# Spectral mixing with three real products: a complex product rebuilt inside a pipelined kernel

## The chip, the core and the metric

The kernel runs on one core of a Trainium2 chip. The metric is the device time of one execution in microseconds (us). A core has a matrix engine (TensorE, in the profile PE for products and PEld for weight loads), a vector engine (VectorE, DVE), a scalar engine (ScalarE, ACT), a general engine (GpSimd, POOL) and SyncE (SP), which here only starts transfers. Each engine works through its own list of instructions in order. Products land in PSUM, which this kernel uses as banks of 512 fp32 columns; everything else lies in SBUF.

## The reference, cut to what matters

```python
def _attn_ref(x, w_r, w_i, b_r, b_i):            # x: 4 batches x 3008 x 256
    X = np.fft.rfft(x, axis=1)
    Xr, Xi = X.real, X.imag
    Yr = Xr @ w_r - Xi @ w_i + b_r               # the mixing: a complex product
    Yi = Xr @ w_i + Xi @ w_r + b_i
    lam = 0.01                                   # soft threshold on both parts
    Yr = np.sign(Yr) * np.maximum(np.abs(Yr) - lam, 0.0)
    Yi = np.sign(Yi) * np.maximum(np.abs(Yi) - lam, 0.0)
    return np.fft.irfft(Yr + 1j * Yi, n=x.shape[1], axis=1)

def _moe_ref(x, w_in, w_out, a, b):              # x: 12032 x 256, 2048 hidden
    h = x @ w_in
    P = a[0] + a[1] * h + a[2] * h**2 + a[3] * h**3
    Q = 1.0 + np.abs(b[0]) * np.abs(h) + np.abs(b[1]) * h**2
    return (P / (Q + 1e-06)) @ w_out
```

The output of the first function, flattened to 12032 rows, is the input of the second.

## The kernel before

The transform of length 3008 is split into 47 x 64. For one batch there are these tasks: eight `f1_task` (the first factor, then a trip through DRAM, `s1`), and then twelve times, for a pair p of frequencies, `f2_task` (the second factor), `m_task` (the mixing with the threshold) and `i1_task` (the first step back, written to DRAM, `s2`). The last step back, `i2_task`, belongs to the second half of the kernel: it makes one block of up to 470 columns of the expert layer's input.

Numbers are kept to nearly fp32 by splitting them into a high and a low fp32r part and multiplying high x high, high x low and low x high (three products); some products are made in plain fp32.

**The mixing.** `f2_task` leaves four pieces of 128 columns in one bank (two frequencies k, two halves dc of the 256 features; in each piece 64 real and 64 imaginary columns). ACT copies the bank to the high part of `x` (L252), DVE subtracts to get the low part (L255), and DVE writes the negated imaginary columns in front of the real ones (L259), so that `-Xi | Xr` can be read as one block of 128 columns. `m_task(b, p, k)` then makes, for one frequency k, twelve products of 256 columns (L283): with `w_r` against `Xr | Xi` and with `w_i` against `-Xi | Xr`, two halves each, three split products each. Its result has real and imaginary rows under each other (64 + 64) and k side by side in the bank. The bank was filled with the two biases beforehand, by a product in batch 0 (L276) and by an ACT copy of `offset` for batches 1 to 3 (L155). After k = 1, ACT (L289) and DVE (L292) apply the threshold and leave `yt`, which `i1_task` multiplies in fp32 by `g1`, two products of 256 columns (L301), whose 128 contracted rows are the real and imaginary rows of one frequency.

**The expert layer** runs over 208 units: 26 blocks of columns by 8 pairs of hidden slices. A unit has 12 products into `h` (`g1_mm`, L385), three passes of ACT over `h` (L417, L418, L421), one adding transfer started by POOL (L419), the polynomial and the quotient on DVE (L433, L434, L442, L444, L454), one subtraction on POOL (L448), and 12 products into `acc` (`g2_mm`, L475), three units later.

**The order.** Batch 0 goes through its tasks before the units start. Those of batches 1 to 3 are laid into the units by a small planner in the main loop. Each task carries `(cost, use, free, generator, part)`; the planner sums the costs that are left and the known cost of each unit up to the batch's deadline (the last unit before its first block), makes a level from them, and at step "F" of each unit starts tasks until the unit's budget is spent. A generator is driven on at later steps: step "e" for tasks of part 0, steps "h"/"m" and the end of the unit for tasks of part 1. What a task must hand to a transfer it appends to `late`, and `flush()` at the start of the next unit issues it on SP. The kernel's last 64 units hold no such tasks; there `alone` is set, and `i2_task` makes the low part with a product (L357) and an ACT copy (L359) instead of DVE's subtraction (L362).

```python
        while cur and spent + cur[0][0] / 2 < budget and held + cur[0][1] <= 2 and not (live and storing(i)):
            cost, use, free, g, part = cur.pop(0)
            next(g, None)
```

Two PSUM banks (tag `ft`) are shared by `f1`, `f2`, mixing, `i1` and `i2`. `h` has two pairs of banks, `acc` two banks.

Of the kernel before, what the change touches and what calls it, by code (L numbers as in the profile page):

```python
# [37 lines left out]
def dft_tables():  # L38
    n2 = np.arange(N2)
    k2 = np.arange(NK)  # L40
    n1 = np.arange(N1)
    k1 = np.arange(N1)
    w = 2.0 * np.pi / N2
    ang = w * ((n2[:, None] * k2[None, :]) % N2)
    f1 = np.zeros((ROWS, NK, 2))
    f1[:N2, :, 0] = np.cos(ang)
    f1[:N2, :, 1] = -np.sin(ang)
    i2b = np.zeros((NK, NG, 2, NG, N2))
    i2 = np.zeros((NK, 2, N2))
# [32 lines left out]
    sel = np.zeros((4, 130))  # L82
    sel[0:2, 0:64] = 1.0
    sel[2:4, 64:128] = 1.0
    sel[0::2, 128] = 1.0
    sel[1::2, 129] = 1.0
    f = np.float32
# [12 lines left out]
def spectral_moe(ctx, tc, t, out):  # L100
# [14 lines left out]
    offset = const.tile([128, 2, D], F32, name="offset")  # L115
    minus = const.tile([128, 128], F32R, name="minus")
    wmix = {n: const.tile([128, 2, D], F32R, name=n) for n in ("wrh", "wrl", "wih", "wil")}
# [20 lines left out]
    def load_x(b, c):  # L138
        if b == 1 and c in (2, 3):
            xt = pro3.tile([128, 4, D], F32, tag=f"x{c}", name="xin", bufs=1)  # L140
        elif b == 1 and c >= 6:
            xt = sm.tile([128, 6, D], F32, tag="x", name="xin", bufs=2)[:, :4]
# [42 lines left out]
    def f1_task(b, c, pos):  # L185
# [11 lines left out]
        elif b > 1:  # L197
            whole = sm.tile([128, 3, 2, D], F32, tag="x", name="a", bufs=2)[:, :NG]
# [41 lines left out]
    def f2_task(b, p):  # L240
# [10 lines left out]
        xs = (sm if b else pro3).tile([128, 2, 4, 192], F32R, tag="x", name="x", bufs=2 if b else 3)  # L251
# [6 lines left out]
        if b or p < 2:  # L258
# [8 lines left out]

    def m_task(b, p, k):
# [4 lines left out]
        if k == 0 and copied:  # L273
            copy(0, pt, offset)
        elif k == 0:
            nc.tensor.matmul(out=pt, lhsT=selr, rhs=bias, start=True, stop=False, skip_group_check=True)  # L276
# [61 lines left out]
    def i2_task(n, ec):  # L338
# [8 lines left out]
        for i in range(JB):  # L347
            z = slice(i * TJ, 512 if i == JB - 1 else (i + 1) * TJ)
# [141 lines left out]
    def fft_tasks(b):  # L490
# [4 lines left out]
        for p in range(np_ + 2):  # L495
# [4 lines left out]
            if 1 <= p <= np_:  # L500
                ts += [(1.43, 1 - k, k, m_task(b, p - 1, k), 0) for k in range(2)]
# [32 lines left out]
    with tc.manual_schedule():  # L534
# [5 lines left out]
        nc.vector.memset(offset[:, 0], 0.0)  # L540
        idle = offset[:, 0].bitcast(mybir.dt.bfloat16)
# [9 lines left out]
        sel = pro.tile([4, 130], F32, tag="sel", name="sel", bufs=1)  # L551
# [11 lines left out]
        def prepare_small():  # L563
            nc.vector.memset(v32(selr), 0.0)
            nc.vector.memset(v32(bias), 0.0)
            yield
            nc.vector.tensor_copy(selr[:4], sel[:, 0:128])
            nc.scalar.activation(out=minus, in_=eye, func=ACTF.Copy)
# [81 lines left out]
        for p in range(np_ + 3):  # L650
# [84 lines left out]
        for i in range(-1, nu + 4):  # L735
# [3 lines left out]
            freed = 0  # L739
            if i == 3:  # L740
# [6 lines left out]
            for step in order.replace("m", "").replace("2", "2m").replace("1A", "Ao1") if nextb == B and not cur else order:  # L747
                if step == "F":
# [14 lines left out]
                    if cur:  # L763
                        budget += plan.pop(0) if plan else level
                        while cur and spent + cur[0][0] / 2 < budget and held + cur[0][1] <= 2 and not (live and storing(i)):
                            cost, use, free, g, part = cur.pop(0)
                            next(g, None)
                            (parts if part else live).append(g)
# [3 lines left out]
                            if not cost:  # L772
# [16 lines left out]
                elif step == "e":  # L789
                    for g in live:  # L790
# [7 lines left out]
            if 0 <= i < nu:  # L798
                dve_a(i)
            next(prev, None)  # L800
# [51 lines left out]
```

## Time and profile before

| | |
|---|---|
| time, median of 3 runs | 1433.52 us (1431.99 to 1437.6) |
| the profiled execution, device time | 1429.0 us |
| its span in the profile | 1427.2 us |
| PE busy / weight loads | 1404.7 us (98%) / 1232.4 us (86%) |
| DVE busy | 1294.8 us (91%) |
| ACT busy | 1135.6 us (80%) |
| POOL busy | 668.9 us (47%) |

How to read it: the profile is of one execution. Busy time is the time in which at least one instruction of the engine is recorded as running. A matmul's record is longer than the distance to the next one's, since they are pipelined, so the chain of waits, which counts from start to start, is the better measure of what a matmul costs. Three stretches can be told apart: batch 0 and the constants (up to about 100 us), units with transform tasks laid in (to about 1060 us), and units without (to the end).

### The profile page before, as it was taken

What the parts mean: (1) busy time and instruction counts of PE and PEld (TensorE: products, weight loads), DVE (VectorE), ACT (ScalarE), POOL (GpSimd) and SP (SyncE); (2) the same over time, 40 slices, a digit from 0 to 9 for tenths busy, and PEclk for the clock granted to TensorE, in tenths of its full rate; (3) what the DMA queues carried; (4) which work ended last, traced back from release to release, by engine and by line L of the source; (5) the groups of instructions that cost most, each with busy time, mean ns of one, the idle gap of its engine ahead of it and who ended that gap; (6) DMA issues with size and microseconds to landing.
All of it is one profiled execution on the core that took longest, in us unless ns stands there. A gap on an engine that the chain in (4) does not pass through costs nothing.

```text
span 1427.2 us, 20352 instructions
## 1 busy us (share of the span) xinstructions
PE 1404.7 (98%) x7525; PEld 1232.4 (86%) x7525; DVE 1294.8 (91%) x1298; ACT 1135.6 (80%) x1439; POOL 668.9 (47%) x444
## 2 busy tenths in 40 slices
PE   9988999999999999999999999999999999999997
PEld 5966999999878999998888999999988888888887
DVE  3868889989899889999889999999999999999998
ACT  3768777788887787878888787888788998888985
POOL 0533444445454444454454444445455555555553
PEclk9999999999999999999999999999999999999999
DMA  9958445546686455546586455555455555555543
GB/s 333 383 189 170 103 104 129 114 89 148 141 205 160 108 108 117 110 102 142 134 213 153 96 122 108 115 116 108 92 124 112 106 115 103 110 113 105 113 80 79
DMA packets 84374, 191.58 MB, mean 134 GB/s; under 512 B 8556, under 2 KB 40468, under 8 KB 84276
## 3 DMA queue, kind: packets, MB, share of 16 engines
q0 software_dynamic: 29952, 98.58, 38.7%
q1 hardware_dynamic: 54212, 91.67, 19.3%
q8 instruction: 59, 0.97, 0.3%
q14 instruction: 39, 0.32, 0.1%
q10 hardware_dynamic: 112, 0.05, 0.0%
HBM read 54.21 MB, written 37.49 MB: 64 GB/s over the span
## 4 chain that ended last, share of the span: by engine, by line
PE 77%; DVE 11%; issue 8%; DMA 2%; ACT 2%; SPq 0%; DVEq 0%; ACTq 0%
PE h L385 29%; PE acc L475 29%; PE pft L283 7%; PE pi L351 4%; DVE t L433 3%; DVE v L444 3%; PE pft L247 2%; PE pft L301 2%; DVE g L442 1%; PE pft L191 1%; PE pft L174 1%; DVE t L434 1%; DVE g L454 1%; PE pm L283 1%; DVE e L525 1%
## 5 line engine op out<-in xcount | busy, mean ns | idle before, releaser
L475 PE MATMUL acc<-g,wsp 128*128 128x470 f32 (+1 forms) x2496 | 562.4, 374 | 3.4 <-DVE g L454 3.4
L448 POOL TENSOR_TENSOR t<-t,v 128x940 f32<-128x940 f32 (+1 forms) x206 | 478.5, 2323 | 137.8 <-DVE v L444 121.5
L475 PEld LDWEIGHTS acc<-g,wsp 128*128 128x128 f32 x2496 | 469.9, 190 | 62.5 <-DVE g L454 4.3
L385 PE MATMUL h<-xsh,win 128*128 128x470 f32 (+1 forms) x1664 | 433.3, 382 | 6.1 <-DVE t L434 5.6
L419 POOL DMA_DIRECT2D v<-s x208 | 183.6, 883 | 538.9 <-issue 501.3
L385 PEld LDWEIGHTS h<-xsh,win 128*128 128x128 f32 x1664 | 304.1, 190 | 61.6 <-PE acc L475 10.9
L417 ACT ACTIVATE v<-h 128x940 f32<-128x940 f32 (+1 forms) x208 | 196.1, 943 | 148.5 <-PE h L385 143.8
L442 DVE SCALAR_TENSOR_TENSOR g<-t,small,y 128x940 fp32r<-128x940 f32 (+1 forms) x208 | 255.2, 1227 | 51.1 <-ACT y L428 48.8
L433 DVE TENSOR_TENSOR t<-t,h 128x940 f32<-128x940 f32 (+1 forms) x208 | 231.4, 1112 | 24.7 <-ACT t L421 22.8
L434 DVE SCALAR_TENSOR_TENSOR t<-t,small,h 128x940 f32<-128x940 f32 (+1 forms) x208 | 245.2, 1179 | 7.4
L454 DVE SCALAR_TENSOR_TENSOR g<-t,small,y 128x940 fp32r<-128x940 f32 (+1 forms) x208 | 244.1, 1174 | 0.1
L385 PE MATMUL h<-xsl,win 128*128 128x470 f32 (+1 forms) x832 | 242.3, 373 | 0.0
L444 DVE SCALAR_TENSOR_TENSOR v<-v,g 128x940 f32<-128x940 f32 (+1 forms) x208 | 231.7, 1114 | 0.0
L421 ACT ACTIVATE t<-h,small 128x940 f32<-128x940 f32 (+1 forms) x208 | 215.6, 1036 | 0.0
L426 ACT ACTIVATE y<-v 128x940 f32<-128x940 f32 (+1 forms) x208 | 205.7, 989 | 8.1 <-DMA v<-s 8.0
L428 ACT ACTIVATE y<-y 128x940 f32<-128x940 f32 (+1 forms) x208 | 203.9, 980 | 2.4
L418 ACT ACTIVATE s<-h 128x940 f32<-128x940 f32 (+1 forms) x208 | 195.3, 939 | 0.0
L385 PEld LDWEIGHTS h<-xsl,win 128*128 128x128 f32 x832 | 156.1, 188 | 19.9
L283 PE MATMUL pft<-wrh,x 128*128 128x256 f32 x288 | 76.7, 288 | 0.2 <-ACT pft L155 0.2
L283 PE MATMUL pft<-wih,x 128*128 128x256 f32 x288 | 75.1, 283 | 0.0
L351 PEld LDWEIGHTS pi<-small,ct 96*128 96x128 f32 x516 | 65.7, 192 | 5.5 <-ACT a L155 3.0
L351 PE MATMUL pi<-small,ct 96*128 96x94 f32 (+1 forms) x516 | 66.9, 277 | 2.1 <-DMA ct<-s 2.1
(90 smaller groups left out, 1070.8 us busy)
## 6 DMA issues: line engine op xcount, KB each, us to landing
v<-s POOLq DMA_DIRECT2D x192, 470.0 KB, 4.5
xin<-in_x SPq DMA_DIRECT2D x30, 512.0 KB, 6.5
s<-zt SPq DMA_DIRECT2D x48, 256.0 KB, 3.5
out_t<-ob SPq DMA_DIRECT2D x48, 235.0 KB, 4.5
ct<-s SPq DMA_DIRECT2D x20, 480.0 KB, 5.5
bt<-s SPq DMA_DIRECT2D x36, 256.0 KB, 3.9
s<-a SPq DMA_DIRECT2D x42, 192.0 KB, 5.2
v<-s POOLq DMA_DIRECT2D x16, 376.0 KB, 4.0
```

Of the source, the lines that this page charges most:

```text
L283: nc.tensor.matmul(out=pt[:, k, :], lhsT=l, rhs=r, start=False, stop=n == len(ops) - 1, skip_group_check=True)
L385: nc.tensor.matmul(out=h[:, i, :w], lhsT=l, rhs=r, start=k == 0, stop=k == len(halves) // FU - 1)
L421: nc.scalar.activation(out=d["t"], in_=h, func=ACTF.Identity, scale=rate["a3"], bias=ca[:, 2:3])
L426: nc.scalar.activation(out=d["y"], in_=d["v"], func=ACTF.Square, bias=C0)
L428: nc.scalar.activation(out=d["y"], in_=d["y"], func=ACTF.Abs_reciprocal_sqrt)
L433: nc.vector.tensor_tensor(out=tt, in0=tt, in1=h, op=ALU.mult)
L434: nc.vector.scalar_tensor_tensor(out=tt, in0=tt, scalar=ca[:, 1:2], in1=h, op0=ALU.add, op1=ALU.mult)
L442: stt(out=hi, in0=tt, scalar=ca[:, 0:1], in1=y, op0=ALU.add, op1=ALU.mult)
L444: stt(out=v, in0=v, scalar=C0, in1=v32(hi), op0=ALU.add, op1=ALU.mult)
L448: nc.gpsimd.tensor_tensor(out=tt[:, :cut], in0=tt[:, :cut], in1=v[:, :cut], op=ALU.subtract)
L454: stt(out=lo, in0=tt, scalar=ca[:, 0:1], in1=y, op0=ALU.add, op1=ALU.mult)
L475: nc.tensor.matmul(out=acc[n][e][:, :w], lhsT=l, rhs=r, start=begun[n] == 1 and seen[e] == 1, stop=begun[n] == UB and seen[e] == 3 * FU)
```

## The change

For batches 1 to 3 the complex product is made from three real ones: with S = (Xr + Xi) w_r, the real part is S - Xi (w_r + w_i) and the imaginary part S + Xr (w_i - w_r). The first of them is made in plain fp32 by a task of its own, `m_sum`: ACT lays `offset` (now `b_r` on all 128 rows) into the first half of a bank, two fp32 products of 256 columns add S, and ACT copies that half to the other half. `m_rest` adds the difference of the biases to the second half by one product (`apart`, `bias`) and then the two other real products in split form, twelve products of 256 columns. Both frequencies k now lie on the rows and the real and imaginary parts side by side, the other way round than `i1_task` needs them, and four transfers of 64 x 256 per pair (`turn`, on SP) bring `yt` to `y`. `f2_task` writes its columns grouped by real and imaginary part; DVE makes the sum and the negated copy is gone. The two new weight matrices are made in unit 0 (`join_mix`) from `w_r` and `w_i`, which are loaded once more during batch 0. In `i2_task` the last product of a block in the stretch without tasks is 94 columns instead of 136. The planner's costs of the two new tasks are 0.86 and 1.56 where the two old ones had 1.43 each, and starting an `m_sum` ends a unit's list of new tasks. Batch 0 keeps `m_task`.

```diff
@@ f2_task
-        pt = bank(b, "f2" if p % 2 else "").rearrange("p (z f) -> p z f", z=4)
+        bank_ = bank(b, "f2" if p % 2 else "")
+        pt = bank_.rearrange("p (z f) -> p z f", z=4)
+        slots = bank_.rearrange("p (c d k j) -> p c d k j", c=2, d=2, k=2)
...
-                nc.tensor.matmul(out=pt[:, 2 * k + dc, :], lhsT=bt[:, k, dc * 128:(dc + 1) * 128],
+                nc.tensor.matmul(out=slots[:, :, dc, k, :] if b else pt[:, 2 * k + dc, :], lhsT=bt[:, k, dc * 128:(dc + 1) * 128],
...
+        if b:
+            total = sm.tile([128, 256], F32, tag="sum", name="total")
+            xs = sm.tile([128, 4, 256], F32R, tag="x", name="x")
+            flat = xs.rearrange("p z f -> p (z f)")
+            nc.scalar.activation(out=total, in_=bank_[:, :256], func=ACTF.Copy)
+            nc.scalar.activation(out=flat[:, :512], in_=bank_, func=ACTF.Copy)
+            yield
+            yield
+            nc.vector.tensor_tensor(out=total, in0=bank_[:, 256:], in1=total, op=ALU.add)
+            nc.vector.tensor_tensor(out=flat[:, 512:], in0=bank_, in1=v32(flat[:, :512]), op=ALU.subtract)
+            yield
+            x_t[b, p] = xs, total
+            return
...
+    def m_sum(b, p):
+        assert copied and not both
+        pt = m_t[b] = bank(b, "m").rearrange("p (c d) -> p c d", c=2)
+        total = x_t[b, p][1]
+        copy(0, pt[:, 0], offset)
+        for dc in range(2):
+            nc.tensor.matmul(out=pt[:, 0], lhsT=total[:, dc * 128:(dc + 1) * 128], rhs=wr[:, dc, :],
+                             start=False, stop=False, skip_group_check=True)
+        both.append(lambda: copy(0, pt[:, 1], pt[:, 0]))
+        yield
+        while both:
+            both.pop()()
+
+    def m_rest(b, p):
...
+        ops = [(1, apart, bias[:, 1])]
+        for c, wh, wl in ((1, "wnh", "wnl"), (0, "wdh", "wdl")):
+            for dc in range(2):
+                ah, al = (xs[:, 2 * z + c, dc * 128:(dc + 1) * 128] for z in range(2))
+                ops += [(1 - c, ah, wmix[wh][:, dc, :]), (1 - c, ah, wmix[wl][:, dc, :]), (1 - c, al, wmix[wh][:, dc, :])]
+        for n, (o, l, r) in enumerate(ops):
+            nc.tensor.matmul(out=pt[:, o], lhsT=l, rhs=r, start=False, stop=n == len(ops) - 1, skip_group_check=True)
+        yield
...
+        def turn():
+            y_t[b, p] = y = sm.tile([128, 2, D], F32, tag="yt", name="y")
+            for k in range(2):
+                for c in range(2):
+                    nc.sync.dma_start(out=y[64 * c:64 * c + 64, k], in_=yt[64 * k:64 * k + 64, c])
+
+        late.append(turn)
+
+    def join_mix(wi):
+        wd = sm.tile([128, 2, D], F32, tag="b", name="wd")
+        nc.vector.tensor_tensor(out=wd, in0=wi, in1=wr, op=ALU.subtract)
+        nc.vector.scalar_tensor_tensor(out=wi, in0=wr, scalar=-1.0, in1=wi, op0=ALU.mult, op1=ALU.subtract)
+        yield
...
+            nc.scalar.activation(out=wmix[h], in_=w, func=ACTF.Copy)
+        yield
+        for w, h, l in ((wi, "wnh", "wnl"), (wd, "wdh", "wdl")):
+            nc.vector.tensor_tensor(out=wmix[l], in0=w, in1=v32(wmix[h]), op=ALU.subtract)
@@ i2_task
-            z = slice(i * TJ, 512 if i == JB - 1 else (i + 1) * TJ)
+            z = slice(i * TJ, 512 if i == JB - 1 and not alone[n] else (i + 1) * TJ)
@@ fft_tasks
-                ts += [(1.43, 1 - k, k, m_task(b, p - 1, k), 0) for k in range(2)]
+                ts += [(0.86, 1, 0, m_sum(b, p - 1), 2), (1.56, 0, 1, m_rest(b, p - 1), 0)]
@@ batch 0, p == 8
-                for k, nm in enumerate(("b_r", "b_i")):
-                    for z in range(2):
-                        nc.sync.dma_start(out=offset[64 * k:64 * k + 64, z],
-                                          in_=t[nm].rearrange("(o d) -> o d", o=1).to_broadcast([64, D]))
+                nc.sync.dma_start(out=offset, in_=t["b_r"].rearrange("(o d) -> o d", o=1).to_broadcast([128, D]))
+                nc.sync.dma_start(out=wr, in_=t["w"][:, 0])
+                w_i = sm.tile([128, 2, D], F32, tag="b", name="w_i")
+                nc.sync.dma_start(out=w_i, in_=t["w"][:, 1])
@@ planner
-                            if not cost:
+                            if not cost or part == 2:
                                 break
```

On PE, in the first half of batch 1's pairs, the mixing of one pair stood as two tasks with a unit's products between them (`h` and `acc` are the units' own products):

```order
L283 MATMUL pft<-wrh,x 128x256
L283 MATMUL pft<-wrl,x 128x256
L283 MATMUL pft<-wrh,x 128x256
L283 MATMUL pft<-wih,x 128x256
L283 MATMUL pft<-wil,x 128x256
L283 MATMUL pft<-wih,x 128x256
L283 MATMUL pft<-wrh,x 128x256
L283 MATMUL pft<-wrl,x 128x256
L283 MATMUL pft<-wrh,x 128x256
L283 MATMUL pft<-wih,x 128x256
L283 MATMUL pft<-wil,x 128x256
L283 MATMUL pft<-wih,x 128x256
```

These are the twelve rows of one frequency; the twelve of the other follow a unit later, or directly. Now, on PE in the same part of the kernel, the start of a mixing reads as follows (L295 the two fp32 products, L457 and L547 the unit's `h` and `acc`, L313 the product for the biases and the first split ones):

```order
L253 MATMUL pft<-f_70,bt 128x2x64 x4
L295 MATMUL pft<-wr,total 128x256 x2
L457 MATMUL h<-xsh,win_489 128x470 x4
L457 MATMUL h<-xsl,win_489 128x470 x2
L457 MATMUL h<-xsh,win_489 128x470 x4
L457 MATMUL h<-xsl,win_489 128x470 x2
L547 MATMUL acc_2296<-g,wsp_1062 128x470 x4
L547 MATMUL acc_2297<-g,wsp_1062 128x470 x4
L547 MATMUL acc_2296<-g,wsp_1062 128x470 x2
L547 MATMUL acc_2297<-g,wsp_1062 128x470 x2
L313 MATMUL pft<-bias,apart 128x256
L313 MATMUL pft<-wnh,x 128x256
```

Eleven more split products follow in the same unit. Between `m_sum` and `m_rest` there is always at least one unit's worth of `h` and `acc`.

On SP, at batch 1's first pairs, this is what stood in its list before (bt: a load for `f2`; s: a store of `i1`; ct: a load for `i2`; out_t: the output):

```order
L227 DMA bt<-s_990 128x2x256 x5
L308 DMA s_1571<-zt 128x2x256
L329 DMA ct<-s_402 96x1280
L227 DMA bt<-s_990 128x2x256 x2
L308 DMA s_1571<-zt 128x2x256
L484 DMA out_t<-ob 128x470 x2
```

And this is what stands at the same place now (y: the turning transfers):

```order
L231 DMA bt<-s_994 128x2x256 x5
L325 DMA y<-yt 64x256 x4
L401 DMA ct<-s_406 96x1280
L325 DMA y<-yt 64x256 x4
L380 DMA s_1669<-zt 128x2x256
L556 DMA out_t<-ob 128x470 x2
L231 DMA bt<-s_994 128x2x256
L325 DMA y<-yt 64x256 x4
L380 DMA s_1669<-zt 128x2x256
```

Per pair, four more entries stand in SP's list, each group behind the DVE instruction that finishes `yt` and, from the second pair of a batch on, behind the previous pair's `i1` products, which read the buffer that `y` takes.

## Rows read from the trace of the kernel before

**Rows 1.** The page's busy times: engine, us, share of the span, instructions.

```profile
PE 1404.7 (98%) x7525; PEld 1232.4 (86%) x7525; DVE 1294.8 (91%) x1298; ACT 1135.6 (80%) x1439; POOL 668.9 (47%) x444
```

**Rows 2.** Busy time of each engine by stretch, and the clock.

```profile
core 0: us, PE busy (x) PEld busy (x) DVE busy (x) ACT busy (x) POOL busy (x), PEclk, DMA share, GB/s
150.00:1050.00 900.00, 900.00 (x4940) 802.78 (x4940) 823.13 (x808) 721.21 (x912) 418.95 (x270) 1.00 0.57 126
900.00:950.00 50.00, 50.00 (x290) 46.79 (x290) 47.86 (x50) 41.14 (x53) 24.04 (x18) 1.00 0.53 112
1150.00:1200.00 50.00, 49.68 (x241) 43.36 (x240) 49.35 (x46) 44.78 (x53) 27.57 (x18) 1.00 0.54 107
```

**Rows 3.** The chain of waits, 264 to 300 us: start, us, what.

```profile
267.39 1.43 PE pft L283 x12
268.82 2.59 PE h L385 x12
271.41 2.57 PE acc L475 x12
273.98 0.86 PE pft L301 x4
274.84 0.89 PE pft L247 x8
...
280.88 1.42 PE pft L283 x12
```

**Rows 4.** Who waited for whom, 150 to 1060 us: total us, times, longest.

```profile
DVE g L442 <- ACT y L428: 48.8, 61, 2.3
...
ACT pft L155 <- DVE xsl L362: 15.3, 8, 2.1
...
ACT pft L155 <- DVE x L255: 12.8, 5, 3.2
PEld h L385 <- DVE v L444: 7.3, 9, 0.8
```

**Rows 5.** Groups by line: shape, count | busy us, mean ns | idle before.

```profile
L255 DVE TENSOR_TENSOR x<-pft,x 128x512 fp32r<-128x512 f32 x48 | 32.7, 682 | 0.8 <-ACT x L252 0.8
...
L155 ACT ACTIVATE pft<-offset 128x512 f32<-128x512 f32 x36 | 21.8, 606 | 35.0 <-DVE xsl L362 18.5 <-DVE x L255 12.8 <-DVE yt L292 3.7
...
L259 DVE TENSOR_SCALAR x<-x 128x512 fp32r<-128x512 f32 x38 | 16.0, 421 | 0.1
...
L359 ACT ACTIVATE xsl<-pi 128x470 fp32r<-128x470 f32 (+1 forms) x14 | 7.7, 552 | 12.7 <-PE pi L357 12.7
...
L568 ACT ACTIVATE minus<-eye 128x128 fp32r<-128x128 f32 x1 | 0.3, 297 | 0.0
```

**Rows 6.** In order of time, one mixing's end and a store (287 to 297 us).

```profile
288.94 0.60 ACT L289 ACTIVATE yt<-pft 128x512 f32<-128x512 f32 x1 [0.33 <-PE pft L283]
...
291.56 0.68 DVE L292 SCALAR_TENSOR_TENSOR yt<-pft,yt 128x512 f32<-128x512 f32 x1
...
296.62 0.38 SPq L308 DMA_DIRECT2D s<-zt  x1
```

**Rows 7.** Transfers: count, KB each, median us from issue to landing.

```profile
xin<-in_x SPq DMA_DIRECT2D x30, 512.0 KB, 6.5
s<-zt SPq DMA_DIRECT2D x48, 256.0 KB, 3.5
```

**Rows 8.** In order of time, units 0 and 1 (99 to 113 us).

```profile
104.15 0.69 DVE L153 COPY a<-pft 128x512 f32<-128x512 f32 x1 [3.72 <-PE pft L191]
...
111.75 0.99 ACT L426 ACTIVATE y<-v 128x940 f32<-128x940 f32 x1 [1.67 <-DMA v<-s]
112.76 0.69 DVE L153 COPY a<-pft 128x512 f32<-128x512 f32 x1 [4.29 <-ACT y L426]
```

**Rows 9.** The chain of waits, 1139 to 1186 us, in the last stretch.

```profile
1142.53 1.13 PE pi L351 x10
...
1175.21 2.81 PE h L385 x12
```

More of the change, by code (lines that the diff above doesn't have):

```diff
@@ L81, in dft_tables @@
     i2p = np.pad(i2b.reshape(96, TJ), ((0, 0), (0, 136 - TJ)))
-    sel = np.zeros((4, 130))
+    sel = np.zeros((4, 258))
     sel[0:2, 0:64] = 1.0
@@ L86, in dft_tables @@
     sel[1::2, 129] = 1.0
+    sel[0:2, 130:] = -1.0
+    sel[2:4, 130:] = 1.0
     f = np.float32
@@ L114, in spectral_moe @@
     bias = const.tile([128, 2, D], F32R, name="bias")
-    offset = const.tile([128, 2, D], F32, name="offset")
+    offset = const.tile([128, D], F32, name="offset")
+    apart = const.tile([128, 128], F32R, name="apart")
+    wr = const.tile([128, 2, D], F32, name="wr")
     minus = const.tile([128, 128], F32R, name="minus")
-    wmix = {n: const.tile([128, 2, D], F32R, name=n) for n in ("wrh", "wrl", "wih", "wil")}
+    wmix = {n: const.tile([128, 2, D], F32R, tag=f"mix{k}", name=n) for k, n in enumerate(("wrh", "wrl", "wih", "wil"))}
     win = {}
@@ L141, in load_x @@
         elif b == 1 and c >= 6:
-            xt = sm.tile([128, 6, D], F32, tag="x", name="xin", bufs=2)[:, :4]
+            xt = sm.tile([128, 4, D], F32, tag="x", name="xin")
         elif b == 0 and c >= 2:
@@ L197, in f1_task @@
         elif b > 1:
-            whole = sm.tile([128, 3, 2, D], F32, tag="x", name="a", bufs=2)[:, :NG]
+            whole = sm.tile([128, NG, 2, D], F32, tag="x", name="a")
         parts = [sm.tile([128, 2, D], F32, tag="a", name="a", bufs=3) if whole is None else whole[:, g] for g in range(NG)]
@@ L266, in spectral_moe @@
     copied = []
+    both = []
+    def m_sum(b, p):
[10 more added lines that the diff above has]
+            both.pop()()
@@ new lines, in m_rest @@
+    def m_rest(b, p):
+        while both:
+            both.pop()()
+        pt = m_t[b]
+        xs = x_t.pop((b, p))[0]
+        ops = [(1, apart, bias[:, 1])]
[6 more added lines that the diff above has]
+        yield
+        fl = lambda z: z.rearrange("p c d -> p (c d)")
+        yt = sm.tile([128, 2, D], F32, tag="yt", name="yt")
+        nc.scalar.activation(out=fl(yt), in_=fl(pt), func=ACTF.Relu, bias=-LAM)
+        yield
+        nc.vector.scalar_tensor_tensor(out=fl(yt), in0=fl(pt), scalar=LAM, in1=fl(yt), op0=ALU.add, op1=ALU.min)
+        def turn():
[4 more added lines that the diff above has]
+        late.append(turn)
@@ new lines, in join_mix @@
+    def join_mix(wi):
[3 more added lines that the diff above has]
+        yield
+        for z, (w, h, l) in enumerate(((wi, "wnh", "wnl"), (wd, "wdh", "wdl"))):
+            for k, n in enumerate((h, l)):
+                wmix[n] = const.tile([128, 2, D], F32R, tag=f"mix{2 * z + k}", name=n)
+            nc.scalar.activation(out=wmix[h], in_=w, func=ACTF.Copy)
+        yield
+        for w, h, l in ((wi, "wnh", "wnl"), (wd, "wdh", "wdl")):
+            nc.vector.tensor_tensor(out=wmix[l], in0=w, in1=v32(wmix[h]), op=ALU.subtract)
@@ L272, in m_task @@
         xs = x_t[b, p]
-        if k == 0 and copied:
-            copy(0, pt, offset)
-        elif k == 0:
+        if k == 0:
             nc.tensor.matmul(out=pt, lhsT=selr, rhs=bias, start=True, stop=False, skip_group_check=True)
@@ L539, in spectral_moe @@
         b_all = [pro3.tile([128, 6, D], F32, tag=f"b{z}", name="b_all", bufs=1) for z in range(4)]
-        nc.vector.memset(offset[:, 0], 0.0)
-        idle = offset[:, 0].bitcast(mybir.dt.bfloat16)
+        nc.vector.memset(offset, 0.0)
+        idle = offset.bitcast(mybir.dt.bfloat16)
         def warm(n, kind=""):
@@ L564, in prepare_small @@
             nc.vector.memset(v32(selr), 0.0)
+            nc.vector.memset(v32(apart), 0.0)
             nc.vector.memset(v32(bias), 0.0)
@@ L567, in prepare_small @@
             nc.vector.tensor_copy(selr[:4], sel[:, 0:128])
+            nc.vector.tensor_copy(apart[:4], sel[:, 130:258])
             nc.scalar.activation(out=minus, in_=eye, func=ACTF.Copy)
@@ L739, in spectral_moe @@
             freed = 0
+            mix = join_mix(w_i) if i == 0 else iter(())
+            next(mix, None)
             if i == 3:
@@ L767, in spectral_moe @@
                             next(g, None)
-                            (parts if part else live).append(g)
+                            (parts if part == 1 else live).append(g)
                             held += use
@@ L789, in spectral_moe @@
                 elif step == "e":
+                    next(mix, None)
                     for g in live:
@@ L799, in spectral_moe @@
                 dve_a(i)
+                drain(mix)
             next(prev, None)
```

6 lines of the change are left out of this document (3 added, 3 removed).

## The prediction

> **What bounds the kernel now.** I read the busy times first, then the engines by stretch, then the chain of waits, then who waits for whom. The busy times [rows 1] put three candidates close together: PE 98%, DVE 91%, weight loads 86%. By stretch [rows 2] they separate: from 150 to 1050 us, where the transforms of batches 1 to 3 are laid into the units, PE is busy 900.00 us of 900 and DVE 823.13, so DVE stands idle for 76.9 us; in the last stretch, without such tasks, both are full (49.68 and 49.35 of 50). The clock there is 1.00 throughout, the 2.4 GHz level. Busy time alone does not say that PE is the limit, since the records of pipelined products overlap. The chain does: between 267 and 282 us [rows 3] it never leaves PE. A unit is 2.59 us of `h`, 2.57 us of `acc`, and what the planner put in: a mixing task (1.43), or an `i1` (0.86) and an `f2` (0.89). The reader should see that the pieces follow each other without a gap. The waits [rows 4] agree: DVE waits 48.8 us for ACT's `y`, but the longest line in which PE's loads wait for DVE is 7.3 us. So in this stretch a microsecond taken from PE is a microsecond of time, until DVE's idle 76.9 us are used up.
>
> **A rule that speaks against this.** The weight loads are busy 802.78 us of 900 (89%) and DVE 91% [rows 2]. The Trainium skill (Perfetto Trace Analysis, Identifying the Most-Contended Engine) calls matmul busy time a poor measure and takes weight-load busy time for TensorE and plain occupancy for DVE, and the highest is to be optimized first. By that DVE is the limit and a change that leaves DVE's work alone gives nothing. The chain [rows 3], which has start-to-start distances and no gap, speaks for PE. The case is kept as a rival below.
>
> **The change, part by part.**
>
> *The products.* Before, one pair costs 1.43 + 1.42 = 2.85 us of PE [rows 3]; 24 products, so 0.119 us each. After, `m_rest` has 13 products of the same shape, 13 x 0.119 = 1.55 us, and `m_sum` two plain fp32 products of 256 columns on full 128 rows, which is exactly what `i1` is: 0.86 us [rows 3]. Together 2.41, saved 0.44 per pair. The ACT copy of the old `offset` was made 36 times [rows 5], once per pair, so 36 x 0.44 = 15.8 us. The price of the fp32 pair is known almost as a row; the other fp32 row, `f2`, has half the columns in four products and costs 0.89, so at worst the saving is 0.41 per pair, 14.8 us. `f2` itself keeps its products; that they now write two runs of 64 columns instead of 128 has no row; I take nothing, and as bounds nothing and a tenth of 0.89 per pair, 3.2 us.
>
> *DVE.* The negated copy goes (0.421 us) and a sum of 256 columns comes. A subtraction from PSUM over 512 costs 0.682 [rows 5]; half of that is 0.34, and fixed cost makes it more; I take 0.42. So DVE's work is unchanged, between -0.08 and +0.26 us per pair. It is off the path with 76.9 us idle.
>
> *ACT.* Before, 512 columns of `offset` cost 0.606. Now there are three copies of 256 (`offset`, one half to the other, the real part into `total`). Between 128 columns at 0.297 and 512 at 0.606 [rows 5], 256 gives 0.40. So ACT gains 3 x 0.40 - 0.606 = 0.6 us per pair, 21 us in all, against 179 us of idle time (900 - 721.21) [rows 2]. It hides, but ACT works in order: what stands behind these copies are the passes over `h` and `y`, for which DVE waits already.
>
> *New waits.* `m_rest` needs ACT's copy of the half bank. It is issued a unit earlier, after the three passes over `h`, and 5.16 us of PE (`h` and `acc`) lie between; it hides. The bank of `f2` is held longer, by one copy of 0.40 and one sum of 0.42; the next `offset` copy or `i1` on that bank waits for it. Before, such ACT waits on DVE came 13 times and took 28.1 us [rows 4], and they reached PE hardly at all. I charge 2.5 us for what now reaches PE, between 0 and 8.
>
> *The turning transfers.* 144 more entries on SP, 0.38 us each to issue by the row of a store [rows 6]: 1.5 us per pair; queued behind them are `bt`, `ct`, stores and outputs, all needed units later. The question is whether `y` is there when `i1` wants it. ACT starts the threshold at 288.94, when the last mixing task, 1.43 us long, has just ended, so that task began at 287.5 [rows 6]; `yt` is finished at 291.56 + 0.68 = 292.24, 4.7 us later. Add 1.5 us to issue and 3.5 to land (a store of the same bytes in one piece) [rows 7]: 9.7 us after `m_rest` begins, 12.7 if it landed as slowly as a 512 KB load (6.5). In the built program `i1` stands two units after its `m_rest` in four of 36 pairs and three to six units after in the others; two units with an `m_rest` in the first are some 13 us. So it hides; the cost is nothing, and at the slow landing at most a microsecond in four places. The transfers that DVE waits for through ACT (`v`) get some company; they hide now.
>
> *Start.* `join_mix` puts four DVE instructions (about 0.68 each) and two ACT copies (0.6 each) into unit 0. DVE sits idle there for 3.72 and 4.29 us [rows 8] around the places where these stand; ACT waited 1.67 us for a transfer in front of L426, more than the 1.2 added. I charge 0.5 us, bounds 0 and 3.9 (all six on the path). The loads of `w_r` and `w_i` are half a load of 512 KB each; at worst one such landing, 6.5 us, which I leave in the upper bound.
>
> *The order.* The planner sees smaller costs and could leave units empty and crowd others. In the built program the 12 pairs of each batch take nearly the same units as before, with the mixing's products now in two tasks of 0.86 and 1.55 that never share a unit, where before some units had both of 1.43. I give it no price.
>
> *The tail.* In the last stretch `i2` has 470 columns instead of 512: 1.13 us [rows 9] x 42/512 = 0.09, in 14 tasks [rows 5], 1.3 us if PE is the limit there, 0 if DVE is; the chain there passes through both. I take 0.6.
>
> *Sum:* -15.8 + 2.5 + 0.5 - 0.6 = -13.4 us, so the profiled execution's 1429.0 would become 1415.6. The median of the runs is 1433.52, 4.5 us above the profiled one; the difference carried over gives 1420.
>
> **The rivals.**
>
> 1. *All of it arrives* (no new wait reaches PE, the tail's share comes): -15.8 - 1.3 = -17.1, 1416.5. For it: 76.9 us of idle DVE and buffers that in the last stretch let PE and DVE run at 99% both. Against: the bank is held longer.
>
> 2. *DVE and ACT become the limit.* DVE is not idle everywhere: at 900 to 950 us it is busy 47.86 of 50 [rows 2]. A third of the saving, batch 3's 5.3 us, lies in such windows; there 2.1 us of 50 are free and 0.9 is asked for. If the order of the engines gives away half of all that is saved, the time is 1433.5 - 7 = 1426.5; if DVE is the limit throughout, 1433.5. By the rule of the Trainium skill weighed in the second paragraph (Perfetto Trace Analysis, Identifying the Most-Contended Engine) the last is the case to expect.
>
> 3. *Slower: ACT is stopped by the longer-held bank.* Place: the `offset` copy at the head of a unit, in front of the passes over `h`. It waits for DVE to empty an `f2` or `i2` bank; 13 waits of 2.2 us on average before [rows 4]. If all 36 did, that is 23 more, 50 us of ACT, and what ACT loses there the next `h` passes and DVE lose too. It decides from the point where more than 13.4 + 7 = 20 us of it reaches PE. With half of it arriving, -13.4 + 25 = +11.6: 1445. Against: ACT has 179 us idle, and the copy is now 0.40 instead of 0.606.
>
> **How the numbers follow.** My forecast's own range is 1416 to 1424 (the waits from 0 to 6, the tail from 0 to 1.3), and I give it 52%. Rival 1 gets 16%, rival 2 half-way 15% and whole (no change) 9%, rival 3 8%. 0.5% is 7.2 us, about what a measurement of this kernel can tell from no change, so the line lies at 1426.3, next to the half-way case, of which I count two thirds as faster. Faster: 52 + 16 + 10 = 78%. Within 0.5%: 5 + 9 = 14%. Slower: rival 3, 8%. The range for 8 in 10 goes from 1412 (all of it arrives, and the two medians are shifted by the spread of the runs) to 1430.
>
> **What would show it.** Right: in the chain, `m_sum` 0.86 and `m_rest` 1.55 as pieces between `h` and `acc`; PE still full from 150 us to the end of the tasks, and that end some 13 us earlier; the sum on DVE near 0.42 and the three ACT copies near 0.40; turning transfers landing in 2 to 4 us, and no PE wait for them. Wrong: an fp32 pair clearly above 0.86; PE idle before `i1` until a transfer; growing waits of DVE for ACT's `y` together with PE loads that wait for DVE; a longer stretch from 60 to 150 us.

## The result and the profile after

| | before | after |
|---|---|---|
| time, median of 5 runs each | 1432.38 us | 1420.63 us (1419.26 to 1424.12) |
| the profiled execution: device time, span | 1429.0, 1427.2 us | 1421.41, 1419.6 us |

The ratio is 0.9918, 95% interval 0.9905 to 0.9932: 11.8 us faster. A repetition of the changed kernel gave 1418.72 us, 0.9902 (0.9887 to 0.9917). The two profiled executions differ by less, 7.6 us, and the first thing to find out is why.

A unit's begin is marked by ACT's first pass over `h`. The next lines are that one instruction in units 5 to 143, the stretch with transform tasks: minimum, median and maximum in ns, and the first and the last start. First the kernel before, then a second profile of it, then the changed kernel.

```profile
L417 ACT ACTIVATE v<-h x139: 782/957/993, 130.1 to 1058.2; 128x940 f32<-128x940 f32 x131, 128x752 f32<-128x752 f32 x8
```

```profile
L417 ACT ACTIVATE v<-h x139: 782/957/993, 133.4 to 1061.5; 128x940 f32<-128x940 f32 x131, 128x752 f32<-128x752 f32 x8
```

```profile
L489 ACT ACTIVATE v<-h x139: 781/957/1003, 134.0 to 1050.5; 128x940 f32<-128x940 f32 x131, 128x752 f32<-128x752 f32 x8
```

The middle stretch takes 1058.2 - 130.1 = 928.1 us in both profiles of before and 1050.5 - 134.0 = 916.5 after (916.4 in the repetition): 11.6 us gone, and it repeats to 0.1 us. What differs from execution to execution is the beginning: unit 5 starts at 130.1 or at 133.4 us in the same kernel. The first profile of before had an early one; that hides 4 us in the comparison of the spans. The last stretch, units 143 to 207, begins and ends as follows, before and after: 349.1 us in both.

```profile
L417 ACT ACTIVATE v<-h x65: 779/957/963, 1058.2 to 1407.3; 128x940 f32<-128x940 f32 x57, 128x752 f32<-128x752 f32 x8
```

```profile
L489 ACT ACTIVATE v<-h x65: 779/957/962, 1050.5 to 1399.6; 128x940 f32<-128x940 f32 x57, 128x752 f32<-128x752 f32 x8
```

So the whole gain lies in the middle. The chain of waits of the changed kernel there (start, us, what) answers to [rows 3]:

```profile
1001.39 0.89 PE pft L253 x8
1002.28 0.87 PE pft L295 x4
1003.15 2.54 PE h L457 x12
1005.69 2.58 PE acc L547 x12
1008.26 1.56 PE pft L313 x13
1009.82 2.59 PE h L457 x12
1012.41 2.58 PE acc L547 x12
1014.98 0.86 PE pft L373 x4
```

In this window it is still PE without a gap. The mixing of a pair is two pieces of 0.87 (`m_sum`) and 1.56 (`m_rest`, 1.54 at other places), where it was 1.43 and 1.42. `f2` (L253) is 0.89 as before, so that its products now write two runs of 64 columns cost nothing.

The busy times, by stretch, answer to [rows 1] and [rows 2]:

```profile
PE 1392.9 (98%) x7273; PEld 1214.9 (86%) x7273; DVE 1290.8 (91%) x1304; ACT 1145.7 (81%) x1513; POOL 667.5 (47%) x444
```

```profile
150.00:1042.00 892.00, 888.30 (x4711) 785.59 (x4710) 819.82 (x814) 732.41 (x984) 417.38 (x270) 1.00 0.62 138
900.00:950.00 50.00, 50.00 (x276) 46.03 (x275) 47.55 (x50) 42.65 (x58) 23.81 (x16) 1.00 0.59 125
1150.00:1200.00 50.00, 49.66 (x241) 43.40 (x240) 49.53 (x46) 44.33 (x53) 27.73 (x19) 1.00 0.56 111
```

PE, which was busy 900.00 of 900 us before, now has 892 - 888.30 = 3.70 us of idle time. Who waited for whom from 150 to 1052 us (total us, times, longest) shows what it waits for, and answers to [rows 4]:

```profile
ACT v L489 <- PE h L457: 67.2, 86, 1.3
DVE g L514 <- ACT y L500: 43.4, 57, 1.8
ACT pft L159 <- DVE x L266: 21.8, 8, 3.7
...
PE pi L423 <- DVE xsl L434: 1.6, 2, 0.9
...
PE pft L253 <- DVE x L266: 0.9, 1, 0.9
...
PE pft L253 <- DMA bt<-s: 0.6, 1, 0.6
...
PE pft L373 <- PE pft L313: 0.4, 1, 0.4
...
PE pft L295 <- ACT pft L159: 0.2, 1, 0.2
```

The five lines of PE add up to those 3.7 us, in six places. In three a task waits for DVE to be done with one of the two `ft` banks. A fourth is the same, though its line names PE: this `i1` starts at 187.34 us, and the subtraction of `f2` (L266) on DVE ended at 186.97. In a fifth `m_sum` waits for the `offset` copy, which waits for such a bank itself. The sixth is a load of `bt`. No product waits for a turning transfer: the one for the `i1` at 187.34 had landed at 181.9.

The idle time understates these stops, since a product's record is longer than the distance to the next one. From start to start (from the fifth product of a unit's `h` to that of the next, less what a median unit and its tasks take) the six units are 5.2 us too long. A unit without a stop became about 0.01 us shorter, 1.2 us over the stretch. Both are estimates from the two traces; together they are the 4 us that are missing from the 15.8 of the forecast's products.

The `offset` copy waits 21.8 us for the subtraction of `f2`, where it waited 12.8 for L255. All its waits together rose from 35.0 [rows 5] to 54.4 us, and the largest part of that is another bank: the one whose last reader is the threshold, L319, 19.1 us where it was 3.7 for L292.

One of the six stops in order of time, on ACT, DVE and PE:

```profile
453.38 0.42 ACT L159 ACTIVATE pft<-pft 128x256 f32<-128x256 f32 x1
453.68 0.41 ACT L261 ACTIVATE total<-pft 128x256 f32<-128x256 f32 x1
453.94 0.63 ACT L262 ACTIVATE x<-pft 128x512 fp32r<-128x512 f32 x1
454.42 1.04 ACT L500 ACTIVATE y<-y 128x940 f32<-128x940 f32 x1
455.49 1.20 DVE L514 SCALAR_TENSOR_TENSOR g<-t,small,y 128x940 fp32r<-128x940 f32 x1 [1.35 <-ACT y L500]
456.60 0.42 DVE L265 TENSOR_TENSOR total<-pft,total 128x256 f32<-128x256 f32 x1
456.93 0.68 DVE L266 TENSOR_TENSOR x<-pft,x 128x512 fp32r<-128x512 f32 x1
457.87 1.13 PE L253 MATMUL pft<-f,bt 128*128 128x128 f32 x8 [0.92 <-DVE x L266]
```

Two new copies (0.30 and 0.26 us from start to start) stand in front of ACT's `y`; DVE waits 1.35 us for that `y`, then makes the new sum (0.33 us) before the subtraction that frees the bank. The three are 0.89 us, as long as PE's wait of 0.92. This is one place in one execution; in the repetition PE waits 0.3 us there.

The operations that the forecast had to estimate (group by line, as in [rows 5]; ACT's three copies and DVE's sum), and the turning transfer (KB, median us to landing; then the issue itself, minimum, median, maximum ns), which answer to [rows 7] and [rows 6]:

```profile
L265 DVE TENSOR_TENSOR total<-pft,total 128x256 f32<-128x256 f32 x36 | 15.0, 417 | 0.0
L261 ACT ACTIVATE total<-pft 128x256 f32<-128x256 f32 x36 | 14.2, 393 | 3.1 <-PE pft L253 3.0
L159 ACT ACTIVATE pft<-pft 128x256 f32<-128x256 f32 x36 | 14.1, 393 | 4.0 <-PE pft L295 3.8
...
L159 ACT ACTIVATE pft<-offset 128x256 f32<-128x256 f32 x36 | 14.1, 392 | 54.4 <-DVE x L266 21.8 <-DVE yt L319 19.1 <-DVE xsl L434 13.5
```

```profile
y<-yt SPq DMA_DIRECT2D x144, 64.0 KB, 2.3
```

```profile
L325 SPq DMA_DIRECT2D y<-yt x144: 461/596/1756, 163.8 to 1037.2; - x144
```

### The profile page after: what moved, and what is told of

Read it like the earlier page. It is cut to its first block, busy times and chain, and to the rows that moved or that the text cites. A ratio compares the mean times of both kernels' runs of the same rounds, so it can differ in the third digit from the quotient of the medians.

```text
span 1419.6 us, 20389 instructions
## 1 busy us (share of the span) xinstructions
PE 1392.9 (98%) x7273; PEld 1214.9 (86%) x7273; DVE 1290.8 (91%) x1304; ACT 1145.7 (81%) x1513; POOL 667.5 (47%) x444
## 5 line engine op out<-in xcount | busy, mean ns | idle before, releaser
L547 PE MATMUL acc<-g,wsp 128*128 128x470 f32 (+1 forms) x2496 | 562.3, 374 | 3.3 <-DVE g L526 3.3
L520 POOL TENSOR_TENSOR t<-t,v 128x940 f32<-128x940 f32 (+1 forms) x206 | 468.7, 2275 | 167.4 <-DVE v L516 146.2
L547 PEld LDWEIGHTS acc<-g,wsp 128*128 128x128 f32 x2496 | 469.7, 189 | 62.5 <-DVE g L526 4.6
L457 PE MATMUL h<-xsh,win 128*128 128x470 f32 (+1 forms) x1664 | 438.5, 385 | 6.5 <-DVE t L506 6.1
L491 POOL DMA_DIRECT2D v<-s x208 | 183.4, 882 | 501.0 <-issue 462.6
L457 PEld LDWEIGHTS h<-xsh,win 128*128 128x128 f32 x1664 | 305.8, 190 | 63.6 <-PE acc L547 10.8
L457 PE MATMUL h<-xsl,win 128*128 128x470 f32 (+1 forms) x832 | 242.3, 373 | 0.0
L493 ACT ACTIVATE t<-h,small 128x940 f32<-128x940 f32 (+1 forms) x208 | 216.2, 1040 | 0.0
L457 PEld LDWEIGHTS h<-xsl,win 128*128 128x128 f32 x832 | 156.4, 189 | 20.1
L159 ACT ACTIVATE pft<-offset 128x256 f32<-128x256 f32 x36 | 14.1, 392 | 54.4 <-DVE x L266 21.8
L253 PEld LDWEIGHTS pft<-f,bt 128*128 128x128 f32 x288 | 37.2, 191 | 3.4 <-ACT s L490 1.1
```

What stands on the lines that cost most here:

```text
L457: nc.tensor.matmul(out=h[:, i, :w], lhsT=l, rhs=r, start=k == 0, stop=k == len(halves) // FU - 1)
L493: nc.scalar.activation(out=d["t"], in_=h, func=ACTF.Identity, scale=rate["a3"], bias=ca[:, 2:3])
L520: nc.gpsimd.tensor_tensor(out=tt[:, :cut], in0=tt[:, :cut], in1=v[:, :cut], op=ALU.subtract)
L547: nc.tensor.matmul(out=acc[n][e][:, :w], lhsT=l, rhs=r, start=begun[n] == 1 and seen[e] == 1, stop=begun[n] == UB and seen[e] == 3 * FU)
```

## The experiments

Each ratio is that of the median to the median of the kernel before on the same chip (1431.9 to 1432.84 us). "Middle" is the distance from unit 5 to unit 143 read as above; "PE idle" is 890 us less PE's busy time from 150 to 1040 us.

| kernel | ratio to before (95%) | middle, us | PE idle, us |
|---|---|---|---|
| before, second profile | | 928.1 | 0.1 |
| after / repeated | 0.9918 (0.9905-0.9932) / 0.9902 (0.9887-0.9917) | 916.5 / 916.4 | 3.7 / 2.8 |
| 20 products per pair | 0.9884 (0.9869-0.9900) | 911.6 | 0.3 |
| more DVE work | 0.9913 (0.9900-0.9927) | 918.6 | 4.7 |
| more ACT work | 0.9937 (0.9925-0.9949) | 919.8 | 5.6 |
| no turning | 0.9910 (0.9897-0.9924) | 915.9 | 3.3 |
| no weight join | 0.9913 (0.9900-0.9926) | 916.8 | 4.1 |
| tail edit alone | 0.9998 (0.9989-1.0006) | 928.6 | 0.4 |
| no unit between | 0.9972 (0.9963-0.9980) | 924.5 | 7.6 |
| sum on POOL | 1.0254 (1.0240-1.0268) | 965.1 | 34.2 |
| half-bank copy on DVE | 0.9917 (0.9903-0.9930) | 917.5 | 7.4 |
| banks freed earlier | 0.9902 (0.9881-0.9923) | 915.6 | 2.7 |

**The changed kernel again.** No edit.

> The changed kernel once more, unchanged, to see what of its start repeats. Theory S (the first 130 us vary from execution to execution): the first pass over h (unit 0) begins anywhere between 103 and 109 us in the new profile, the stretch from unit 5 to the end of the tasks again lasts 916 to 917 us, and the ratio to the kernel before is again 0.990 to 0.993. Rival C (the change costs the start 4 us): unit 0 begins again near 108 us.

The middle came out 0.1 us from the first profile. Two edits below that were meant for the ends alone (no weight join, tail edit) moved it by 0.3 and 0.5 us, so differences of 1 us in it can be read, and smaller ones not safely. The ends of the execution are looser. Five of the six stops recur; the one of `m_sum` doesn't.

**Is PE the limit? 20 products instead of 24, in the kernel before.**

```diff
+        if b:
+            del ops[4], ops[1]
```

> The kernel before with 20 instead of 24 mixing products per pair in batches 1 to 3 (two high-times-low products of each frequency are left out, so the values are a little less exact); nothing else changes, the planner's costs neither. 4 x 0.119 us x 36 = 17.2 us of PE. Theory PE (the products set the time there): 14 to 17 us faster, ratio 0.988 to 0.990. Rival DVE (vector is the limit): 0 to 4 us faster, ratio 0.997 or more.

The products taken out are 36 x 4 x 0.119 = 17.2 us. The middle fell from 928.1 to 911.6, by 16.5 us, with DVE's and ACT's work unchanged:

```profile
L419 ACT ACTIVATE v<-h x139: 782/957/997, 132.0 to 1043.6; 128x940 f32<-128x940 f32 x131, 128x752 f32<-128x752 f32 x8
```

96% of what was taken from PE was saved in time. This decides against DVE as the limit, and it shows that what the change lost on the way (11.6 arrived of 15.8) isn't a limit that any saving would have met, but something that comes with its other parts.

**DVE loaded by one more copy per pair (L268, 419 ns, 15.1 us in all).**

```diff
+            nc.vector.tensor_scalar(out=flat[:, 512:], in0=v32(flat[:, 512:]), scalar1=1.0, scalar2=None, op0=ALU.mult)
```

> The changed kernel with one more DVE instruction per pair, in the place where the negated copy stood (the low part multiplied by 1, 512 columns in SBUF, 0.42 us, 15 us in all). Theory PE: hidden, 0 to 3 us slower than the changed kernel. Rival DVE: 12 to 15 us slower, which would give back the whole gain.

Of 15.1 us of work 2.1 reached the middle. DVE has room there; it isn't free.

**ACT loaded by one more copy per pair (the `offset` copy made twice, 14 us in all).**

```diff
+        copy(0, pt[:, 0], offset)
         copy(0, pt[:, 0], offset)
```

> The changed kernel with the copy of the offset made twice per pair: one more ACT instruction of 0.39 us at the head of 36 units, 14 us of ACT. Theory PE: hidden in ACT's idle time, 0 to 3 us slower than the changed kernel. Rival ACT (what stands at the head of ACT's unit holds up the passes over h, then DVE, then PE): 8 to 14 us slower.

3.3 us of 14 reached the middle, a quarter. So this place in ACT's list is dearer than the one tried in DVE's, although ACT's busy share is lower (81% against 91%). Other places in either list weren't tried. Part of it is direct: `m_sum` now waits for the doubled copy itself, 1.3 us in three places.

**Without the turning transfers.**

```diff
-        late.append(turn)
+        y_t[b, p] = yt
```

> The changed kernel without the turning transfers: the first step back reads the threshold's result as it lies (so what is computed there is not the reference's). Theory PE: the transfers are hidden, 0 to 1 us faster than the changed kernel. Rival T (the 144 transfers disturb the others and SP's list): 3 us faster or more, with fewer waits of ACT for v and of PE before i2 and f2.

0.6 us less in the middle, too little to be read safely, and no change in the whole time that the measurement can tell. The transfers are hidden, as forecast. The wait of `f2` for a load of `bt` (0.6 us) is absent here; no turning transfer was issued in the 25 us before that wait in the changed kernel, so that they cause it isn't shown.

**Without the making of the new weights.**

```diff
-        for c, wh, wl in ((1, "wnh", "wnl"), (0, "wdh", "wdl")):
+        for c, wh, wl in ((1, "wrh", "wrl"), (0, "wih", "wil")):
...
-            mix = join_mix(w_i) if i == 0 else iter(())
+            mix = iter(())
```

> The changed kernel without join_mix and without the second load of the imaginary weights (the mixing then multiplies by the weights of batch 0, so its values are not the reference's): four DVE instructions and two ACT copies fewer in unit 0, 256 KB less to load. Theory hidden: the stretch from unit 0 to unit 5 (26.1 us in both profiles of the changed kernel, 26.8 before) and the time stay within 1 us. Rival start: unit 5 comes 2 to 4 us earlier.

No change in the time. Unit 5 begins at 133.4 us, within the spread that both kernels show without this edit.

**The tail edit alone, in the kernel before.**

```diff
-            z = slice(i * TJ, 512 if i == JB - 1 else (i + 1) * TJ)
+            z = slice(i * TJ, 512 if i == JB - 1 and not alone[n] else (i + 1) * TJ)
```

> The kernel before with the shorter last product of i2 in the stretch without tasks (94 columns, not 136), and nothing else of the change. From the last task to the last unit the kernel before takes 344.5 us. Theory DVE-tail (DVE sets the period of that stretch): 344.3 to 344.7 and no change of the time. Rival PE-tail: 343.2, 1.3 us less.

Nothing: its last stretch, too, is 349.1 us:

```profile
L417 ACT ACTIVATE v<-h x65: 778/957/963, 1061.4 to 1410.5; 128x940 f32<-128x940 f32 x57, 128x752 f32<-128x752 f32 x8
```

In that stretch an `i2` piece of the changed kernel's chain is 1.09 us where it was 1.13 [rows 9], so 14 of them give PE 0.6 us, and the stretch does not get shorter: here a small saving on PE is worth nothing.

```profile
1083.86 1.09 PE pi L423 x10
```

**`m_rest` may follow `m_sum` in the same unit.**

```diff
-                            if not cost or part == 2:
+                            if not cost:
```

> The changed kernel, with the planner no longer ending a unit's list after an m_sum, so that m_rest can follow it in the same unit. Theory W (the unit between hides ACT's copy from one half bank to the other): wherever both fall into one unit PE waits for a copy of 0.4 us, its start and the semaphores, about 0.7 us each; if 20 of 36 pairs do, 10 to 15 us slower than the changed kernel. Rival: the copy was never in the way; 0 to 2 us.

Most of the gain goes: 1427.82 us against 1420.63, and the middle is 8.0 us longer. The waits name it (150 to 1052 us):

```profile
ACT pft L159 <- PE pft L295: 23.0, 15, 4.0
...
PEld pft L313 <- ACT pft L159: 6.9, 8, 0.9
...
PE pft L313 <- ACT pft L159: 3.7, 8, 0.5
```

In eight places `m_rest` now stands waiting for the copy from one half of the bank to the other, and ACT, which must make that copy in its turn, is itself held 23.0 us for `m_sum` (3.8 in the changed kernel). Counted from start to start as above, nine units of the middle hold both tasks (one lies before 150 us), and each is 0.7 to 1.0 us too long, 7.4 us in all. The price per place is about the expected one, the number of places nine and not twenty. One line of the planner carries two thirds of the gain.

**The sum on POOL, from SBUF.** This tests whether the bank of `f2`, which the sum holds longer, is what the lost 4 us are.

```diff
-            nc.scalar.activation(out=total, in_=bank_[:, :256], func=ACTF.Copy)
...
-            nc.vector.tensor_tensor(out=total, in0=bank_[:, 256:], in1=total, op=ALU.add)
...
+            nc.gpsimd.tensor_tensor(out=total, in0=v32(xs[:, 2]), in1=v32(xs[:, 3]), op=ALU.add)
+            for z in range(2):
+                nc.gpsimd.tensor_tensor(out=total, in0=total, in1=v32(xs[:, z]), op=ALU.add)
```

> The changed kernel with the sum of real and imaginary part made on POOL from the split parts in SBUF (three additions of 256 columns) instead of by an ACT copy and a DVE addition from the bank, so that f2's bank is held no longer than before. ACT has 0.4 and DVE 0.42 us less per pair, POOL some 2 us more, between its transfers and its subtraction for the units. Theory bank (the 4 us of new PE waits come from the longer-held bank): 2 to 4 us faster than the changed kernel. Rival POOL (POOL's subtraction comes later, DVE waits, then PE): the same or slower.

A miss: 2.5% slower than before. The groups of POOL's own additions, and then the waits (150 to 1052 us):

```profile
L268 POOL TENSOR_TENSOR total<-total,x 128x256 f32<-128x256 f32 x72 | 80.8, 1123 | 5.6
L266 POOL TENSOR_TENSOR total<-x 128x256 f32<-128x256 f32 x36 | 58.0, 1610 | 69.4 <-DVE x L264 67.7 <-ACT ob L159 1.7
```

```profile
POOL total L266 <- DVE x L264: 63.7, 33, 2.8
ACT y L499 <- DMA v<-s: 49.5, 35, 4.3
...
PE pft L296 <- ACT pft L159: 10.2, 8, 2.2
```

Three additions are 3.86 us per pair, and the first of them waits for DVE, 33 times, with the rest of POOL's list behind it. POOL is also the engine that starts the adding transfer of every unit (L491 before this edit), so these start late, and ACT waits 49.5 us for them (15.0 in the changed kernel). The question of the bank wasn't answered by this run, because a queue was in its way.

**The half-bank copy on DVE, with the bias in it.** The copy between the halves becomes DVE's addition of the difference of the biases; one product per pair and one ACT copy go.

```diff
-        both.append(lambda: copy(0, pt[:, 1], pt[:, 0]))
+        both.append(lambda: nc.vector.tensor_tensor(out=pt[:, 1], in0=pt[:, 0], in1=gap, op=ALU.add))
+        yield
...
-        ops = [(1, apart, bias[:, 1])]
+        ops = []
```

> The changed kernel with the difference of the biases brought in by DVE: it writes the second half of the bank as the first plus a row of differences (256 columns, about 0.4 us, at the end of the unit), in place of ACT's copy and of the first product of m_rest. PE has 36 x 0.12 = 4.3 us less, ACT 14 us less, DVE 15 us more; the planner's cost of m_rest is 1.44. Theory PE: 3 to 6 us faster than the changed kernel, since ACT is relieved as well. Rival DVE: 0, or slower.

No gain. The 36 products are 4.3 us less of PE, and PE stands idle 3.7 us more. (The planner's cost of `m_rest` went to 1.44 with them.) The waits (150 to 1052 us):

```profile
PEld pft L312 <- DVE pft L295: 6.9, 8, 1.8
...
PE pft L312 <- DVE pft L295: 4.1, 5, 1.4
```

DVE makes the addition behind a unit's polynomial, later than ACT made its copy, and in five places `m_rest` waits for it.

**The banks freed earlier.** Same instructions, same engines; the sum reads the copy in SBUF, behind the last reader of the bank.

```diff
-            nc.scalar.activation(out=total, in_=bank_[:, :256], func=ACTF.Copy)
             nc.scalar.activation(out=flat[:, :512], in_=bank_, func=ACTF.Copy)
+            nc.scalar.activation(out=total, in_=v32(flat[:, :256]), func=ACTF.Copy)
...
-            nc.vector.tensor_tensor(out=total, in0=bank_[:, 256:], in1=total, op=ALU.add)
             nc.vector.tensor_tensor(out=flat[:, 512:], in0=bank_, in1=v32(flat[:, :512]), op=ALU.subtract)
+            nc.vector.tensor_tensor(out=total, in0=v32(flat[:, 256:512]), in1=total, op=ALU.add)
```

> The same number of instructions on every engine as after, in another order: ACT's 256-column copy for the sum and DVE's sum read the SBUF copy of x instead of the bank, behind the last reader of the bank (ACT's copy, DVE's subtraction), so that each f2 bank is free some 0.4 us (ACT) and some 0.42 us (DVE) earlier. Left out: the low part of Xr + Xi in the first of the three products. Theory bank: the 4 us that the middle stretch lost (start to start of ACT's first pass, units 5 to 143: 916.5 us, against 928.1 - 15.8 = 912.3) are PE and ACT waiting for banks that are held longer; then the waits of the offset copy for the subtraction (21.8 us, 8 times) shrink to about half, PE's idle time of 3.7 us in the stretch falls to 2 or less, and the stretch to 913 to 915. Rival order: it is the order of ACT and DVE work within a unit (more instructions in front of the passes over h), whoever holds a bank; then the stretch stays at 916 to 917.5. Rival work: only the amount matters; also no change.

Neither side's number in full: the middle fell by 0.9 us, to 915.6, and PE's idle time from 3.7 to 2.7 by the table (2.8 in the repetition of the unedited kernel). The wait of the `offset` copy, which the theory wanted halved, hardly moved:

```profile
ACT pft L159 <- DVE x L265: 19.1, 8, 3.1
```

So freeing the bank behind the subtraction gives back 0.9 us, about a fifth of the 4.2. It isn't a clean price: in the new order ACT's first pass over `h` waits 10.0 us for POOL, where it waited 2.0. PE's two stops before `i2` fell from 1.6 to 1.2 us in all; at the one shown above PE waits 0.6 us, between the 0.9 and the 0.3 of the unedited kernel's two profiles. For the rest the rows of that stop and the loads (2.1 us for 15.1 of DVE, 3.3 for 14 of ACT) point to ACT's order: two copies per pair more than before, in front of the passes over `h` and `y`. No run takes these copies out alone, so this part stays argued, not shown.

## Why the prediction was right, step by step

- **What bounds it.** PE in the middle stretch: shown by the 20-product kernel (16.5 of 17.2 us arrive), and the chain agrees. The rule of the Trainium skill weighed there (Perfetto Trace Analysis, Identifying the Most-Contended Engine) pointed at DVE with its 91%; the traces disagree, since 15.1 us more of DVE cost 2.1. In the last stretch the tail run shows the opposite: there a small saving on PE is worth nothing.
- **The products**, -15.8 us: 0.87 and 1.54 to 1.56 against 0.86 and 1.55 forecast. `f2`'s runs of 64 columns: 0.89 against 0.89. Right.
- **DVE and ACT**: the sum 0.417 against 0.42, ACT's copies 0.392 to 0.393 against 0.40. Right.
- **New waits**, +2.5 us: too small by 1.7, inside its bounds of 0 to 8. 15.8 us of products and 11.6 in the middle leave 4.2, and by the estimate above they lie in the six stops. The place was right for the bank of `f2`, held longer by a copy and a sum. Not priced were the copies as such, though the prediction says that they stand in front of passes for which DVE waits; the waits for the mixing's own bank (3.7 us [rows 5], now 19.1), which its count of ACT's 13 waits leaves out, didn't enter either. What each of these gave of the 4.2 us is open.
- **Turning transfers**, nothing: right in the result. The step to it was off: an issue was taken as 0.38 us and took 0.60 in the median, and the landing took 2.3 instead of 3.5; the two errors have opposite signs.
- **Start**, +0.5 us: nothing that can be told from its own spread (unit 5 begins between 129.7 and 134.0 us over all kernels).
- **The tail**, -0.6 us: nothing. The chain there passed through both engines, which was taken as half a limit; a saving on PE alone gave none. The saving itself was 0.04 us per task and not 0.09.
- **The order**: no price was given, and the unit that always lies between the two tasks turned out to be worth 8 us. The forecast rested on it without saying so in the sum.
- **The sum**: -15.8 + 4.2 = -11.6 instead of -13.4. That the time came closer (1420.0 forecast, 1420.63 measured) is luck: the median shown of before, 1433.52, was 1.1 us above that of all five runs.
- **Rivals.** All arrives: not so, by 4 us and the tail (by its own terms it gives 1416.4, not 1416.5). DVE as the limit: refuted by the load on DVE and the 20-product kernel; ACT: by the load on ACT. Slower by the longer-held bank: the waits are there (ACT's `offset` copy 54.4 us against 35.0), but all that was lost is 4 us and not 25; the POOL run shows what it looks like when ACT is really stopped.

## What to carry to other kernels

Where one engine's chain had no gap over hundreds of microseconds, as here, a product taken out was worth nearly its start-to-start distance, and two engines at 80 to 90% beside it did not change that. Helper work laid on those two cost 14 to 24% of its length, and not evenly: PE stopped in six places without it and in eight with it, mostly before a bank that DVE had not emptied. So look for the places, not for the busy share. When a product is split into a part and a rest with another engine between them, try an order that puts a whole unit between the two: here that was two thirds of the gain. And compare stretches between the same instructions of two traces, not spans of single executions: the start alone moved by up to 4 us.

## What was not expected of the hardware

The beginning differs between executions of one kernel, in part by the granted clock. The stretch from 95 to 109 us (columns as in [rows 2]), first before, then after:

```profile
95.00:109.00 14.00, 12.04 (x62) 8.58 (x63) 6.26 (x8) 7.63 (x12) 3.73 (x4) 0.88 0.76 216
```

```profile
95.00:109.00 14.00, 11.89 (x52) 8.64 (x49) 6.45 (x11) 5.30 (x10) 3.04 (x2) 0.63 0.66 205
```

0.63 is a mean of the two levels, 2.4 and 1.2 GHz. In order of time, the same task in before, its second profile, after and its repetition:

```profile
96.28 2.87 PE L351 MATMUL pi<-small,ct 96*128 96x94 f32 x20 [2.12 <-DMA ct<-s]
```

```profile
98.09 4.13 PE L351 MATMUL pi<-small,ct 96*128 96x94 f32 x20 [2.15 <-DMA ct<-s]
```

```profile
98.19 4.66 PE L423 MATMUL pi<-small,ct 96*128 96x94 f32 x20 [2.11 <-DMA ct<-s]
```

```profile
98.66 2.68 PE L423 MATMUL pi<-small,ct 96*128 96x94 f32 x20 [2.17 <-DMA ct<-s]
```

The twenty products take between 2.68 and 4.66 us, each time behind 2.1 us in which PE waits for `ct`. The granted clock of the stretch goes with it: 0.88, 0.76, 0.63 and 0.88 in this order, so it isn't the change. Of the changed kernel's two profiles, whose unit 5 starts 2.4 us apart, these products account for 2.0 us. Of the 3.3 us between the two of before they account for 1.3; 1.8 had been lost before they began. After 150 us the clock was 1.00 in before and after.

On POOL an addition of 256 fp32 columns took 1.12 us where it read the running sum and a piece of `x`, and 1.61 in the first of the three, which reads two pieces of `x` (DVE: 0.417 for a sum of the same shape, one source in PSUM). Whether DVE's work beside it has a part in this wasn't separated.
